# A mixture-of-experts kernel behind linear attention: layer 1 of all four experts in another seven-product form

## Chip, core and metric

One Trainium2 chip, of which the kernel uses one core. The metric is the device time of one execution in microseconds (us). Before the change it is 514.11 us, the median of three runs (513.86 to 515.35).

## What is computed

Linear attention feeds a small mixture of experts. The reference, cut to what matters:

```python
def phi(x): return np.where(x > 0, x, np.exp(x) - 1.0) + 1.0
q_p, k_p = phi(q), phi(k)                       # 8 batches, 8 heads, 576 tokens, 64 wide
kv  = einsum('bhsd,bhse->bhde', k_p, v); z = k_p.sum(axis=2)
x   = einsum('bhsd,bhde->bhse', q_p, kv) / (einsum('bhsd,bhd->bhs', q_p, z)[..., None] + 1e-6)
x   = x as (4608 tokens, 512)
p   = domain_probs / (domain_probs.sum(-1, keepdims=True) + 1e-9)
for e in range(4):
    h = np.maximum(x @ w1[e], 0.0)              # 512 -> 1024
    out += p[:, e:e+1] * (h @ w2[e])            # 1024 -> 512
```

## The kernel before

**Stages.** Attention of the first batches runs on its own, with its loads; the first 512 tokens of the experts (`first_l1`, `first_l2`) lie between its parts. The rest of the experts is cut into 64 units: `units` goes over j from 1 to 8 (512 tokens each), two halves s of 256 tokens, and the four experts e, which turn fastest. Beside the units, attention of batches 2 to 7 runs until about 370 us.

**One unit.** A unit is two token tiles of 128 (t = 0, 1) for one expert. ScalarE scales x by the token's share p into `xp` (L649, two instructions), the DMA queue of SyncE transposes it into `xT` (L651). Layer 1 makes h, layer 2 multiplies it with w2 and adds into four PSUM banks `l2b`, which stay open over the four experts; after expert 3 the output sums (L832 to L841) go to `ot` and to memory.

**Seven products.** Both layers are 2 x 2 block products: x as x[t, k] (token tile t, half k of the 512), w1 as quadrants q[f, k] (half f of the 1024, half k), h as h[t, f]. Eight block products give four results; with sums of blocks, seven do. A block product on TensorE is 8 matmuls of 128 columns. `l1_seven` does so for experts 0 to 2, with three PSUM banks that turn from unit to unit: the first product A is read by ScalarE, which writes its negative into bank W (L717), so that the third product adds onto it; the second, Bk, is copied to `m2` (L719). VectorE takes W - m2 to `w` (L722). Products four and five end in relus on ScalarE (L725, L728), six and seven in VectorE instructions that add `w` and cut off below zero (L731, L735). `l1_plain` does expert 3 with all eight block products (L747: 32 matmuls of 256 columns, four relus L766). Layer 2 is in seven products for all experts: `ssums` makes four sums of h on VectorE (L785), `l2_unit` seven products of four matmuls of 256 columns (L799), in the order that `seq` gives.

**Weight sums.** `sums_w1` makes on VectorE three new tiles `w1x` for each of the experts 0 to 2 and overwrites quadrants of w1 in place, six instructions in all (L487, L498). The in-place ones have to wait until the first 512 tokens, which use the plain w1, are through.

**Sums of x.** `xsums` (L661 to L668) makes five sums in three instructions for a unit of experts 0 to 2.

**What sets the order.** Everything is first noted in a plan: `pl.add(engine, duration, priority, function, reads, writes)`. `Plan.order` then plays the plan with these durations (0.45 us for a layer-1 product, 0.436 for a layer-2 one, 0.5 for a PSUM read on ScalarE, 0.55 for an x scaling, 0.62 for a VectorE read of PSUM) and 0.28 us from engine to engine. At each step the engine that can start first takes, of what is ready, the one with the lowest priority number. The result is a fixed order for each engine. Priorities are due times: unit n is due at

```python
T0, TU = 84.0, 6.4
U = lambda n: T0 + n * TU
```

a layer-1 product i of unit n at U(n) + 0.9 i, a layer-2 product i of the same unit at U(n+1) + 0.45 + 0.9 i, so that layer 1 of one unit interleaves with layer 2 of the one before. In fact an engine doesn't wait for a due time; it takes what is ready.

**Loads.** The first two batches use three staging buffers for k, q and v; the third lies on tiles that units use later (`w` and `m2`). Outputs turn over three `ot` tiles.

Of the kernel before, what the change touches and what calls it, by code (L numbers as in the profile page):

```python
# [10 lines left out]
FP32 = mybir.dt.float32  # L11
FP16 = mybir.dt.float16
# [97 lines left out]
def kernel(  # L110
# [16 lines left out]
    P = 128  # L127
# [10 lines left out]
    SEVEN1 = (0, 1, 2)  # L138
# [13 lines left out]
    w1x = {e: sb(f"w1x_{e}", [P, 3, 2, FH], FP16) for e in SEVEN1}  # L152
# [5 lines left out]
    xp_b = [sb(f"xp{i}", [P, 2, Dm], FP16) for i in range(2)]  # L158
    xT_b = [sb(f"xT{i}", [P, 2, DC, P], FP16) for i in range(3)]
    xs_b = [sb(f"xs{i}", [P, 5, 2, P], FP16) for i in range(2)]  # L160
    h_b = [sb(f"h{i}", [P, 2, 2, HF, P], FP16) for i in range(2)]
    s4_b = [sb(f"s4{i}", [P, 4, HF, P], FP16) for i in range(2)]
    m2_b = sb("m2", [P, 512], FP32)
    w_b = sb("w", [P, 2, 512], FP32)
    s15 = sb("s15", [P, 2, HD], FP32)
    ot_b = [sb(f"ot{i}", [P, 2, Dm], FP32) for i in range(3)]
# [17 lines left out]
    kqs.append(w_b.rearrange("p a (i h c d) -> p (a i) h c d", i=1, h=2, c=C))  # L184
    vss.append(m2_b.rearrange("p (h c d) -> p h c d", h=2, c=C))
# [24 lines left out]
    def stage_keys(i):  # L210

        if i < 2:
            return ("st", i, 0), ("st", i, 1), ("st", i, 2)
        return ("w", 0), ("w", 1), ("m2",)
# [61 lines left out]
    def probs():  # L276
        raw = sb("praw", [P, B, C, E], FP32)
        rrest = sb("prawr", [P, B // 2, E], FP32)
        src = moe_domain_probs.rearrange("(b s) e -> s b e", s=S)
        dma("POOL", 6, raw, src[0:NT].rearrange("(p c) b e -> p b c e", c=C), ("praw",), 1.5)  # L280
        for par in range(2):
            dma("POOL", 6, rrest[par * R : (par + 1) * R],
                src[NT:S].rearrange("s (b t) e -> t s b e", t=2)[par], (("prawr", par),), 0.4)

        def go(r, o, rs, nb):
            nc.vector.tensor_reduce(out=rs, in_=r, axis=mybir.AxisListType.X, op=AO.add)
            nc.vector.tensor_scalar(rs, rs, 1e-9, None, AO.add)
            nc.vector.reciprocal(rs, rs)
            nc.vector.scalar_tensor_tensor(
                out=o, in0=r, scalar=INV, in1=rs.broadcast_to([P, nb, E]),  # L290
                op0=AO.mult, op1=AO.mult,
            )

        rs0, rs1 = sb("prs0", [P, B * C], FP32), sb("prs1", [P, B // 2], FP32)
        pl.add("DVE", 0.6, 24, lambda: go(raw.rearrange("p b c e -> p (b c) e"),
               p_nat.rearrange("p b c e -> p (b c) e"), rs0, B * C), r=("praw",), w=("pnat",))
        pl.add("DVE", 0.4, 60, lambda: go(rrest, p_rest, rs1, B // 2),
               r=(("prawr", 0), ("prawr", 1)), w=("prest",))
# [179 lines left out]
    def sums_w1(e, pri):  # L478

        if e not in SEVEN1:  # L480
            return
# [7 lines left out]
        q00, q01, q10, q11 = wq(e, 0, 0), wq(e, 0, 1), wq(e, 1, 0), wq(e, 1, 1)  # L489
        for o, a, b_, alu, r, w in (  # L490
            (w1x[e][:, 2], q00, q01, AO.add, K(0, 0) + K(0, 1), (X(2),)),
            (w1x[e][:, 1], q10, q11, AO.add, K(1, 0) + K(1, 1), (X(1),)),
            (w1x[e][:, 0], q00, q11, AO.add, K(0, 0) + K(1, 1), (X(0),)),
            (q10, q10, q00, AO.subtract, K(0, 0), K(1, 0)),
            (q01, q01, q11, AO.subtract, K(1, 1), K(0, 1)),
        ):
            pl.add("DVE", 0.62, pri, two(o, a, b_, alu), r=r, w=w, after=22)
        pl.add("DVE", 0.4, pri, lambda: nc.vector.tensor_scalar(q00, q00, -1.0, None, AO.mult),  # L498
               r=(), w=K(0, 0))
# [155 lines left out]
    def xsums(n):  # L655
        if units[n][2] not in SEVEN1:
            return
# [3 lines left out]
        for i, (o, a, b_, alu, dur, d) in enumerate((  # L661
            (xs[:, 4], xT[:, 0, 0:2], xT[:, 1, 2:4], AO.add, 0.25, 1.8),
            (xs[:, 2:4], xT[:, :, 2:4], xT[:, :, 0:2], AO.subtract, 0.42, 2.7),
            (xs[:, 0:2].rearrange("p a k t -> p (a k) t"), xT[:, 0], xT[:, 1], AO.add, 0.42, 4.5),
        )):
            pl.add("DVE", dur, U(n) + d - 1.0,
                   lambda o=o, a=a, b_=b_, alu=alu: tt(out=o, in0=a, in1=b_, op=alu),  # L667
                   r=(("xT", ti),), w=(("xs", xi, i),))  # L668
# [4 lines left out]
    def l1_seven(n):  # L673
# [3 lines left out]
        i0 = rot("l1u", 3)  # L677
        cnt["l1u"] += 1
        ia, ib, iw = i0, (i0 + 1) % 3, (i0 + 2) % 3
        A, Bk, W = l1b[ia], l1b[ib], l1b[iw]  # L680
        ka, kb, kw = "l1b%d" % ia, "l1b%d" % ib, "l1b%d" % iw
        wi = n % 2
        w = w_b[:, wi]
        H = lambda t, f: ("h", n % 2, t, f)
        K = lambda i, kk: k1(e, i, kk)
        X = lambda i: ("w1x", e, i)

        def prod(bank, wt, r, start):
# [12 lines left out]
        t_ = (("xT", ti),)  # L701
        steps = (
            (A, ka, w1x[e][:, 2], (X(2),), xT[:, 1, 2:4], t_, True),
            (Bk, kb, w1x[e][:, 1], (X(1),), xT[:, 0, 0:2], t_, True),
            (W, kw, w1x[e][:, 0], (X(0),), xs[:, 4], x_(0), False),
            (A, ka, wq(e, 0, 0), K(0, 0), xs[:, 3], x_(1), False),
            (Bk, kb, wq(e, 1, 1), K(1, 1), xs[:, 2], x_(1), False),
            (A, ka, wq(e, 1, 0), K(1, 0), xs[:, 0], x_(2), False),
            (Bk, kb, wq(e, 0, 1), K(0, 1), xs[:, 1], x_(2), False),
        )  # L710
        for i, (bank, key, wt, wkey, r, rk, start) in enumerate(steps):
# [3 lines left out]
                   r=rk + wkey, w=(key,))  # L715
            if i == 0:
                pl.add("ACT", 0.5, p_ + 1.0, lambda: nc.scalar.mul(W, A, -1.0), r=(ka,), w=(kw,))  # L717
            elif i == 1:
                pl.add("ACT", 0.5, p_ + 1.0, lambda: nc.scalar.copy(m2_b, Bk),  # L719
                       r=(kb,), w=(("m2",),))  # L720
            elif i == 2:
                pl.add("DVE", 0.62, p_ + 1.5, lambda: nc.vector.tensor_tensor(  # L722
                    out=w, in0=W, in1=m2_b, op=AO.subtract), r=(kw, ("m2",)), w=(("w", wi),))
            elif i == 3:
                pl.add("ACT", 0.5, p_ + 0.9, lambda: nc.scalar.activation(  # L725
                    hq(n, 1, 0), A, AF.Relu), r=(ka,), w=(H(1, 0),))
            elif i == 4:
                pl.add("ACT", 0.5, p_ + 0.9, lambda: nc.scalar.activation(  # L728
                    hq(n, 0, 1), Bk, AF.Relu), r=(kb,), w=(H(0, 1),))
            elif i == 5:  # L730
                pl.add("DVE", 0.62, p_ + 0.5, lambda: nc.vector._custom_dve(  # L731
                    TENSOR_ADD_SAT, out=hq(n, 1, 1), in0=A, in1=w, s0=BIG, s1=0.0),
                    r=(ka, ("w", wi)), w=(H(1, 1),))
            else:
                pl.add("DVE", 0.62, p_ + 0.5, lambda: nc.vector._custom_dve(  # L735
                    TENSOR_ADD_SAT, out=hq(n, 0, 0), in0=Bk, in1=w, s0=BIG, s1=0.0),
                    r=(kb, ("w", wi)), w=(H(0, 0),))

    def l1_plain(n):
        j, s, e = units[n]  # L740
        ti = n % 3
        xT = xT_b[ti]
        h = h_b[n % 2]

        def prod(ph, fp, f2):
            for dc in range(DC):
                nc.tensor.matmul(  # L747
                    out=ph[:, f2 * 2 * P : (f2 + 1) * 2 * P],
                    lhsT=w1_sb[e][:, dc, (2 * fp + f2) * P : (2 * fp + f2 + 1) * P],
                    rhs=xT[:, :, dc, :],  # L750
                    start=(f2 == 0 and dc == 0),
                    stop=(dc == DC - 1),
                    skip_group_check=True,
                )

        for fp in range(FC // 2):
            bi = rot("l1u", 3)
            ph, key = l1b[bi], "l1b%d" % bi
            f, c0 = (2 * fp) // HF, (2 * fp) % HF
            for f2 in range(2):  # L760
                pl.add("PE", 0.436, U(n) + 1.6 * fp + 0.8 * f2,
                       lambda ph=ph, fp=fp, f2=f2: prod(ph, fp, f2),
                       r=(("xT", ti),) + k1(e, (2 * fp) // HF, 0) + k1(e, (2 * fp) // HF, 1),
                       w=(key,))
            pl.add("ACT", 0.52, U(n) + 1.6 * fp + 1.5,
                   lambda ph=ph, f=f, c0=c0: nc.scalar.activation(  # L766
                       h[:, :, f, c0 : c0 + 2, :],
                       ph.rearrange("p (c u t) -> p u c t", c=2, u=2),
                       AF.Relu), r=(key,), w=(("h", n % 2, 0, f), ("h", n % 2, 1, f)))
# [18 lines left out]
    def l2_unit(n):  # L788
# [26 lines left out]
        seq = (P2, P4, P1, P5, P6, P7, P3)  # L815
        if first:
            seq = (P2, P1, P5, P6, P7, P4, P3)
# [7 lines left out]
        oi = rot("ot", 3)  # L825
# [98 lines left out]
    for n in range(nu):  # L924
# [5 lines left out]
        (l1_seven if units[n][2] in SEVEN1 else l1_plain)(n)  # L930
# [45 lines left out]
```

## Time and profile before

| | |
|---|---|
| median of three runs | 514.11 us |
| the profiled execution | 514.07 us |
| its span, first to last instruction | 512.2 us |
| mean granted clock of TensorE | 0.996 |
| TensorE busy (PE) | 486.8 us |
| VectorE busy (DVE) | 411.8 us |
| ScalarE busy (ACT) | 333.7 us |
| first product of unit 0 starts | 85.1 us |
| last layer-2 product ends | 504.4 us |
| L691, 128-wide matmuls of seven-product layer 1 | 2688 |
| L747, 256-wide matmuls of plain layer 1 | 512 |

How to read it: the profile gives each engine's busy time, groups of instructions by source line with count, busy sum, mean duration in ns and the idle time before them, and who ended that idle time. The chain of work that ended last is followed back from the last instruction. A timeline row has the start, the duration, the engine, the line, what is written and read, and how many instructions it joins. A matmul's end is modelled and includes the drain of the pipeline, so back-to-back matmuls overlap in these rows; their starts tell the pace. PEld is the loading of weights, which lies under matmuls.

### The profile page before, as it was taken

The numbers are of one execution on the slowest core, as the hardware profiler recorded it, in microseconds if no ns is written. First come the engines' busy times: TensorE is split into PE (matmuls) and PEld (weight loads), VectorE is DVE, ScalarE is ACT, GpSimd is POOL, SyncE is SP. The second block draws the span as 40 slices with busy tenths as digits, with TensorE's granted clock in tenths as the row PEclk, the third lists the DMA queues.
The fourth block names the chain that finished last, engine by engine and source line by source line (L and its number), as shares of the span: only waits on it lengthen the run. The fifth ranks groups of instructions, "written<-read, shape, count | busy, mean of one in ns | idle before, by whom it ended". The sixth has DMA issues, their size and how long they took to land.

```text
span 512.2 us, 13906 instructions
## 1 busy us (share of the span) xinstructions
PE 486.8 (95%) x5624; PEld 424.3 (83%) x5624; DVE 411.8 (80%) x1005; ACT 333.7 (65%) x621; POOL 42.8 (8%) x68
## 2 busy tenths in 40 slices
PE   1889998999999999999999999999999999999993
PEld 0444544899999999999999999999999999999993
DVE  5887987989898989898989889888877675767652
ACT  5638568878885688658765886578546756565431
POOL 8756400000000000000000000000000000000000
PEclk9999999999999999999999999999999999999998
DMA  8999988996565587455745475735423224232211
GB/s 230 240 231 235 262 182 183 243 196 158 115 176 109 153 144 154 115 155 125 171 115 134 113 176 102 148 91 102 76 42 85 49 77 57 70 60 66 53 33 42
DMA packets 124001, 67.44 MB, mean 132 GB/s; under 512 B 94480, under 2 KB 117776, under 8 KB 123936
## 3 DMA queue, kind: packets, MB, share of 16 engines
q1 hardware_dynamic: 115216, 51.79, 46.4%
q0 software_dynamic: 8720, 14.76, 13.4%
q8 instruction: 44, 0.72, 0.6%
q14 instruction: 21, 0.17, 0.1%
HBM read 45.16 MB, written 9.44 MB: 107 GB/s over the span
## 4 chain that ended last, share of the span: by engine, by line
PE 90%; DVE 3%; ACT 2%; DMA 2%; issue 1%; POOL 0%; POOLq 0%; DVEq 0%; ACTq 0%
PE l2b L799 37%; PE l1b L691 28%; PE l1b L747 11%; PE l2b L547 5%; PE l1b L537 5%; PE at L421 2%; PE at L397 1%; DMA vr<-in_v_dram 1%; DMA xT<-xp 1%; DVE x L437 0%; ACT ek L355 0%; ACT xp L649 0%; PE l2b L367 0%; PE at L400 0%; DVE ot L839 0%
## 5 line engine op out<-in xcount | busy, mean ns | idle before, releaser
L691 PE MATMUL l1b<-xs,w 128*128 128x128 f16 x1536 | 116.0, 219 | 1.4 <-ACT h L725 1.4
L799 PE MATMUL l2b<-t,s 128*128 128x256 f16 x768 | 114.6, 273 | 0.1
L799 PE MATMUL l2b<-w,h 128*128 128x256 f16 x768 | 113.6, 273 | 0.2 <-DVE h L731 0.2
L691 PEld LDWEIGHTS <-w 128*128 128x128 f16 x1536 | 100.2, 98 | 5.3 <-issue 1.5
L799 PEld LDWEIGHTS <-s 128*128 128x128 f16 x1024 | 92.5, 98 | 7.8 <-DVE s L785 0.3
L649 ACT ACTIVATE xp<-x,p_nat 128x512 f16<-128x512 f16 x112 | 76.5, 719 | 3.4 <-DMA xT<-xp 3.2
L691 PEld LDWEIGHTS <-w1x 128*128 128x128 f16 x1152 | 75.2, 98 | 3.9 <-DVE xs L667 0.9
L785 DVE TENSOR_TENSOR s<-h 128x512 f16<-128x512 f16 x128 | 53.8, 420 | 27.7 <-ACT h L766 27.1
L799 PEld LDWEIGHTS <-h 128*128 128x128 f16 x768 | 69.5, 98 | 6.4 <-DVE h L731 0.3
L747 PE MATMUL l1b<-xT,w 128*128 128x256 f16 x512 | 74.0, 273 | 0.0
L766 ACT ACTIVATE h<-l1b 128x512 f16<-128x512 f32 x64 | 38.1, 595 | 45.8 <-PE l1b L747 40.4
L691 PE MATMUL l1b<-xT,w1x 128*128 128x128 f16 x768 | 57.6, 219 | 0.0
L747 PEld LDWEIGHTS <-w 128*128 128x128 f16 x512 | 49.6, 98 | 5.5
L667 DVE TENSOR_TENSOR xs<-xT 128x256 f16<-128x256 f16 x144 | 48.3, 374 | 6.8 <-PE l1b L691 4.7
L725 ACT ACTIVATE h<-l1b 128x512 f16<-128x512 f32 x48 | 28.5, 594 | 32.3 <-PE l1b L691 32.3
L717 ACT ACTIVATE l1b<-l1b 128x512 f32<-128x512 f32 x48 | 28.1, 586 | 21.3 <-PE l1b L691 15.5
L355 ACT ACTIVATE ek<-kq 128x512 f16<-128x512 f32 x60 | 37.6, 631 | 6.3 <-DVE kqp L348 2.5
L731 DVE CUSTOM_DVE_ANT_0 h<-l1b,w 128x512 f16<-128x512 f32 x48 | 32.9, 686 | 10.4 <-ACT h L728 5.0
L722 DVE TENSOR_TENSOR w<-l1b,m 128x512 f32<-128x512 f32 x48 | 32.9, 686 | 7.3 <-PE l1b L691 6.3
L799 PE MATMUL l2b<-w,s 128*128 128x256 f16 x256 | 38.4, 273 | 0.0
L735 DVE CUSTOM_DVE_ANT_0 h<-l1b,w 128x512 f16<-128x512 f32 x48 | 33.0, 687 | 2.1 <-PE l1b L691 0.9
L348 DVE TENSOR_TENSOR kqp<-ek,kqp 128x512 f16<-128x512 f16 x64 | 27.2, 426 | 9.0 <-ACT ek L355 5.2
(100 smaller groups left out, 621.0 us busy)
## 6 DMA issues: line engine op xcount, KB each, us to landing
w<-in_moe_w_dram POOLq DMA_DIRECT2D x32, 256.0 KB, 7.4
out_dram<-ot SPq DMA_DIRECT2D x16, 512.0 KB, 3.0
kq<-in_k_dram SPq DMA_DIRECT2D x25, 256.0 KB, 3.2
vs<-in_v_dram SPq DMA_DIRECT2D x25, 256.0 KB, 3.2
kq<-in_q_dram SPq DMA_DIRECT2D x25, 256.0 KB, 3.0
kq<-in_k_dram POOLq DMA_DIRECT2D x5, 256.0 KB, 7.2
vs<-in_v_dram POOLq DMA_DIRECT2D x5, 256.0 KB, 6.6
kq<-in_q_dram POOLq DMA_DIRECT2D x5, 256.0 KB, 6.1
```

What stands on the lines that cost most here:

```text
L355: pl.add("ACT", 0.55, pri + i * step, lambda i=i: nc.scalar.activation(ek[:, i], kq[:, i], AF.Exp), r=(sk[i],), w=(("ek", ei, i),))
L649: pl.add("ACT", 0.55, pri, lambda c=c, src=src, ps=ps: nc.scalar.activation(xp[:, c, :], src, AF.Copy, scale=ps), r=r, w=(("xp", xi, c),))
L667: lambda o=o, a=a, b_=b_, alu=alu: tt(out=o, in0=a, in1=b_, op=alu),
L691: nc.tensor.matmul(out=bank[:, fc * P : (fc + 1) * P], lhsT=wt[:, kc, fc * P : (fc + 1) * P], rhs=r[:, kc, :], start=(start and fc == 0 an ...
L722: pl.add("DVE", 0.62, p_ + 1.5, lambda: nc.vector.tensor_tensor(out=w, in0=W, in1=m2_b, op=AO.subtract), r=(kw, ("m2",)), w=(("w", wi),))
L725: pl.add("ACT", 0.5, p_ + 0.9, lambda: nc.scalar.activation(hq(n, 1, 0), A, AF.Relu), r=(ka,), w=(H(1, 0),))
L731: pl.add("DVE", 0.62, p_ + 0.5, lambda: nc.vector._custom_dve(TENSOR_ADD_SAT, out=hq(n, 1, 1), in0=A, in1=w, s0=BIG, s1=0.0), r=(ka, ("w", ...
L735: pl.add("DVE", 0.62, p_ + 0.5, lambda: nc.vector._custom_dve(TENSOR_ADD_SAT, out=hq(n, 0, 0), in0=Bk, in1=w, s0=BIG, s1=0.0), r=(kb, ("w" ...
L747: nc.tensor.matmul(out=ph[:, f2 * 2 * P : (f2 + 1) * 2 * P], lhsT=w1_sb[e][:, dc, (2 * fp + f2) * P : (2 * fp + f2 + 1) * P], rhs=xT[:, :, ...
L766: lambda ph=ph, f=f, c0=c0: nc.scalar.activation(h[:, :, f, c0 : c0 + 2, :], ph.rearrange("p (c u t) -> p u c t", c=2, u=2), AF.Relu), r=( ...
L785: pl.add("DVE", 0.36, U(n + 1) + d - 0.5, lambda i=i, a=a, b_=b_, alu=alu: tt(out=s4[:, i], in0=a, in1=b_, op=alu), r=r, w=(Q(i),))
L799: nc.tensor.matmul(out=l2b[bank][:, half * HD : (half + 1) * HD], lhsT=a[:, c, :], rhs=w[:, c], start=(opens and first and c == 0), stop=( ...
```

## The change

Layer 1 of all four experts takes one form of seven products, another than before, and `l1_plain` goes. With sums of weights

w1 = q10 + q11, w2 = w1 - q00, w4 = q01 - w2, and q10 overwritten by q00 - q10

(four instructions for each of four experts) and four sums of x in three instructions, each of which uses the one before, the seven products go into the banks X, Y, Z:

1. X = q00 x00; ScalarE copies X to Y.
2. Z = w1 xs0; ScalarE copies Z to `p5`.
3. X += w2 xs2; ScalarE copies X to `u2`.
4. Y += q01 x01; ScalarE: h[0,0] = relu(Y).
5. X += (q00 - q10) xs1; VectorE: h[1,1] = relu(X + p5).
6. Z += w4 x11; VectorE: h[1,0] = relu(Z + u2).
7. X += q11 xs3; ScalarE: h[0,1] = relu(X).

In the next unit X and Y change places. The subtraction L722 goes; ScalarE reads PSUM five times in a unit in place of four. Layer 2 takes its products in another order (P1 before P4 before P5). The third staging buffer lies on `xp` and `u2`, the raw probabilities on `p5`, and `ot` has two tiles in place of three. The core of the diff:

```diff
-    SEVEN1 = (0, 1, 2)
-    w1x = {e: sb(f"w1x_{e}", [P, 3, 2, FH], FP16) for e in SEVEN1}
+    w1x = [sb(f"w1x_{e}", [P, 3, 2, FH], FP16) for e in range(E)]
-    m2_b = sb("m2", [P, 512], FP32)
-    w_b = sb("w", [P, 2, 512], FP32)
+    u2_b = [sb(f"u2{i}", [P, 512], FP32) for i in range(2)]
+    p5_b = sb("p5", [P, 512], FP32)
-    ot_b = [sb(f"ot{i}", [P, 2, Dm], FP32) for i in range(3)]
+    ot_b = [sb(f"ot{i}", [P, 2, Dm], FP32) for i in range(2)]
...
+            (w1, q10, q11, AO.add, K(1, 0) + K(1, 1), (X(0),)),
+            (w2, w1, q00, AO.subtract, (X(0),) + K(0, 0), (X(1),)),
+            (w4, q01, w2, AO.subtract, (X(1),) + K(0, 1), (X(2),)),
+            (q10, q00, q10, AO.subtract, K(0, 0), K(1, 0)),
...
+            (xs[:, 0:2], xT[:, 1].rearrange("p (a k) t -> p a k t", a=2), xT[:, :, 0:2],
+             0.42, 0.9, (), (X(0), X(1))),
+            (xs[:, 2], xT[:, 1, 2:4], xs[:, 0], 0.25, 1.8, (X(0),), (X(2),)),
+            (xs[:, 3], xT[:, 0, 2:4], xs[:, 2], 0.25, 5.4, (X(2),), (X(3),)),
...
+        ix, iy, iz = cnt.get("l1u", (0, 1, 2))
+        cnt["l1u"] = (iy, ix, iz)
...
+            (X, kx, wq(e, 0, 0), k1(e, 0, 0), xT[:, 0, 0:2], t_, True,
+             ("ACT", 0.5, 1.0, copy(Y, X), (kx,), (ky,))),
+            (Z, kz, w1, S_(0), xs[:, 0], x_(0), True,
+             ("ACT", 0.5, 2.5, copy(p5_b, Z), (kz,), ("p5",))),
+            (X, kx, w2, S_(1), xs[:, 2], x_(2), False,
+             ("ACT", 0.5, 1.0, copy(u2, X), (kx,), (("u2", ui),))),
+            (Y, ky, wq(e, 0, 1), k1(e, 0, 1), xT[:, 0, 2:4], t_, False,
+             ("ACT", 0.5, 2.0, relu(hq(n, 0, 0), Y), (ky,), (H(0, 0),))),
+            (X, kx, wq(e, 1, 0), k1(e, 1, 0), xs[:, 1], x_(1), False,
+             ("DVE", 0.62, 0.9, relu2(hq(n, 1, 1), X, p5_b), (kx, "p5"), (H(1, 1),))),
+            (Z, kz, w4, S_(2), xT[:, 1, 2:4], t_, False,
+             ("DVE", 0.62, 1.2, relu2(hq(n, 1, 0), Z, u2), (kz, ("u2", ui)), (H(1, 0),))),
+            (X, kx, wq(e, 1, 1), k1(e, 1, 1), xs[:, 3], x_(3), False,
+             ("ACT", 0.5, 1.0, relu(hq(n, 0, 1), X), (kx,), (H(0, 1),))),
...
-        seq = (P2, P4, P1, P5, P6, P7, P3)
+        seq = (P1, P4, P5, P2, P6, P7, P3)
         if first:
-            seq = (P2, P1, P5, P6, P7, P4, P3)
+            seq = (P1, P5, P2, P6, P7, P4, P3)
...
-        oi = rot("ot", 3)
+        oi = rot("ot", 2)
```

The third number in each tuple after "ACT" or "DVE" is how long after the product's due time the reader is due.

More of the change, by code (lines that the diff above doesn't have):

```diff
@@ L156 @@
     p_rest = sb("p_rest", [P, B // 2, E], FP32)
-    xp_b = [sb(f"xp{i}", [P, 2, Dm], FP16) for i in range(2)]
+    xp_a = sb("xp", [P, 2, 2, Dm], FP16)
+    xp_b = [xp_a[:, i] for i in range(2)]
     xT_b = [sb(f"xT{i}", [P, 2, DC, P], FP16) for i in range(3)]
-    xs_b = [sb(f"xs{i}", [P, 5, 2, P], FP16) for i in range(2)]
+    xs_b = [sb(f"xs{i}", [P, 4, 2, P], FP16) for i in range(2)]
     h_b = [sb(f"h{i}", [P, 2, 2, HF, P], FP16) for i in range(2)]
     s4_b = [sb(f"s4{i}", [P, 4, HF, P], FP16) for i in range(2)]
-    m2_b = sb("m2", [P, 512], FP32)
-    w_b = sb("w", [P, 2, 512], FP32)
+    u2_b = [sb(f"u2{i}", [P, 512], FP32) for i in range(2)]
+    p5_b = sb("p5", [P, 512], FP32)
     s15 = sb("s15", [P, 2, HD], FP32)
-    ot_b = [sb(f"ot{i}", [P, 2, Dm], FP32) for i in range(3)]
+    ot_b = [sb(f"ot{i}", [P, 2, Dm], FP32) for i in range(2)]
     kqs = [sb(f"kq{i}", [P, 2, 2, C, D], FP32) for i in range(2)]
@@ L182 @@
     xr_sb = sb("xr_sb", [P, B // 2, Dm], FP16)
-    kqs.append(w_b.rearrange("p a (i h c d) -> p (a i) h c d", i=1, h=2, c=C))
-    vss.append(m2_b.rearrange("p (h c d) -> p h c d", h=2, c=C))
+    kqs.append(
+        xp_a.bitcast(FP32).rearrange("p a c (x d) -> p a (c x) d", d=D)
+        .rearrange("p a (h c) d -> p a h c d", h=2)
+    )
+    vss.append(u2_b[0].rearrange("p (h c d) -> p h c d", h=2, c=C))
     xt0 = s4_b[1].rearrange("p a c t -> p a (c t)")
@@ L213, in stage_keys @@
             return ("st", i, 0), ("st", i, 1), ("st", i, 2)
-        return ("w", 0), ("w", 1), ("m2",)
+        return ("xp", 0), ("xp", 1), ("u2", 0)
     last = {}
@@ L276, in probs @@
     def probs():
-        raw = sb("praw", [P, B, C, E], FP32)
+        raw = p5_b[:, 0 : B * C * E].rearrange("p (b c e) -> p b c e", b=B, c=C)
         rrest = sb("prawr", [P, B // 2, E], FP32)
         src = moe_domain_probs.rearrange("(b s) e -> s b e", s=S)
-        dma("POOL", 6, raw, src[0:NT].rearrange("(p c) b e -> p b c e", c=C), ("praw",), 1.5)
+        dma("POOL", 6, raw, src[0:NT].rearrange("(p c) b e -> p b c e", c=C), ("p5",), 1.5)
         for par in range(2):
@@ L295, in probs @@
         pl.add("DVE", 0.6, 24, lambda: go(raw.rearrange("p b c e -> p (b c) e"),
-               p_nat.rearrange("p b c e -> p (b c) e"), rs0, B * C), r=("praw",), w=("pnat",))
+               p_nat.rearrange("p b c e -> p (b c) e"), rs0, B * C), r=("p5",), w=("pnat",))
         pl.add("DVE", 0.4, 60, lambda: go(rrest, p_rest, rs1, B // 2),
@@ L478, in sums_w1 @@
     def sums_w1(e, pri):
-        if e not in SEVEN1:
-            return
         tt = nc.vector.tensor_tensor
@@ L489, in sums_w1 @@
         q00, q01, q10, q11 = wq(e, 0, 0), wq(e, 0, 1), wq(e, 1, 0), wq(e, 1, 1)
+        w1, w2, w4 = (w1x[e][:, i] for i in range(3))
         for o, a, b_, alu, r, w in (
[L491 to L495, printed above, removed]
+            (w1, q10, q11, AO.add, K(1, 0) + K(1, 1), (X(0),)),
+            (w2, w1, q00, AO.subtract, (X(0),) + K(0, 0), (X(1),)),
+            (w4, q01, w2, AO.subtract, (X(1),) + K(0, 1), (X(2),)),
+            (q10, q00, q10, AO.subtract, K(0, 0), K(1, 0)),
         ):
             pl.add("DVE", 0.62, pri, two(o, a, b_, alu), r=r, w=w, after=22)
-        pl.add("DVE", 0.4, pri, lambda: nc.vector.tensor_scalar(q00, q00, -1.0, None, AO.mult),
-               r=(), w=K(0, 0))
     def sums_w2(e, pri):
@@ L655, in xsums @@
     def xsums(n):
-        if units[n][2] not in SEVEN1:
-            return
         xi, ti = n % 2, n % 3
@@ L660, in xsums @@
         tt = nc.vector.tensor_tensor
[L661 to L664, printed above, removed]
+        X = lambda i: ("xs", xi, i)
+        for i, (o, a, b_, dur, d, r, w) in enumerate((
+            (xs[:, 0:2], xT[:, 1].rearrange("p (a k) t -> p a k t", a=2), xT[:, :, 0:2],
+             0.42, 0.9, (), (X(0), X(1))),
+            (xs[:, 2], xT[:, 1, 2:4], xs[:, 0], 0.25, 1.8, (X(0),), (X(2),)),
+            (xs[:, 3], xT[:, 0, 2:4], xs[:, 2], 0.25, 5.4, (X(2),), (X(3),)),
         )):
             pl.add("DVE", dur, U(n) + d - 1.0,
-                   lambda o=o, a=a, b_=b_, alu=alu: tt(out=o, in0=a, in1=b_, op=alu),
-                   r=(("xT", ti),), w=(("xs", xi, i),))
+                   lambda o=o, a=a, b_=b_: tt(out=o, in0=a, in1=b_, op=AO.subtract),
+                   r=(("xT", ti),) + r, w=w)
     def hq(n, t, f):
@@ L676, in l1_seven @@
         xT, xs = xT_b[ti], xs_b[xi]
[L677 to L683, printed above, removed]
+        ix, iy, iz = cnt.get("l1u", (0, 1, 2))
+        cnt["l1u"] = (iy, ix, iz)
+        X, Y, Z = l1b[ix], l1b[iy], l1b[iz]
+        kx, ky, kz = "l1b%d" % ix, "l1b%d" % iy, "l1b%d" % iz
+        ui = n % 2
+        u2 = u2_b[ui]
         H = lambda t, f: ("h", n % 2, t, f)
-        K = lambda i, kk: k1(e, i, kk)
-        X = lambda i: ("w1x", e, i)
+        S_ = lambda i: (("w1x", e, i),)
         def prod(bank, wt, r, start):
@@ L701, in l1_seven, with relu, copy, relu2 @@
         t_ = (("xT", ti),)
-        steps = (
[L703 to L709, printed above, removed]
+        w1, w2, w4 = (w1x[e][:, i] for i in range(3))
+        def relu(o, bank):
+            return lambda: nc.scalar.activation(o, bank, AF.Relu)
+        def copy(o, bank):
+            return lambda: nc.scalar.copy(o, bank)
+        def relu2(o, bank, t):
+            return lambda: nc.vector._custom_dve(
+                TENSOR_ADD_SAT, out=o, in0=bank, in1=t, s0=BIG, s1=0.0
+            )
+        steps = (
+            (X, kx, wq(e, 0, 0), k1(e, 0, 0), xT[:, 0, 0:2], t_, True,
[12 more added lines that the diff above has]
+             ("ACT", 0.5, 1.0, relu(hq(n, 0, 1), X), (kx,), (H(0, 1),))),
         )
-        for i, (bank, key, wt, wkey, r, rk, start) in enumerate(steps):
+        for i, (bank, key, wt, wk, r, rk, start, then) in enumerate(steps):
             p_ = U(n) + 0.9 * i
@@ L714, in l1_seven @@
                    lambda bank=bank, wt=wt, r=r, start=start: prod(bank, wt, r, start),
[L715 to L769, printed above, removed]
@@ L771, in ssums @@
+                   r=rk + wk, w=(key,))
+            eng, dur, d, f, r, w = then
+            pl.add(eng, dur, p_ + d, f, r=r, w=w)
     def ssums(n):
@@ L929 @@
         xsums(n)
-        (l1_seven if units[n][2] in SEVEN1 else l1_plain)(n)
+        l1_seven(n)
         ssums(n)
```

## Prediction

> **What bounds the kernel now.** I read the busy shares first, then the waits of TensorE, then busy time by stretch, then the timeline of single units, last the rows of the instructions that the change adds and removes.
>
> ```profile
> PE 486.8 (95%) x5624; PEld 424.3 (83%) x5624; DVE 411.8 (80%) x1005; ACT 333.7 (65%) x621; POOL 42.8 (8%) x68
> ...
> PE 90%; DVE 3%; ACT 2%; DMA 2%; issue 1%; POOL 0%; POOLq 0%; DVEq 0%; ACTq 0%
> ```
>
> TensorE (PE) is busy for 95% and carries 90% of the chain that ended last. The waits of PE show where the rest goes:
>
> ```profile
> PE l1b L691 <- ACT h L725: 1.4, 1, 1.4
> ...
> PE l1b L691 <- DVE xs L667: 0.8, 1, 0.8
> ```
>
> These two, both in unit 0, are all that layer 1 waited for (waits under 150 ns aren't listed). Busy time by stretch (PE, weight loads, VectorE = DVE, ScalarE = ACT):
>
> ```profile
> 185.00:210.00 25.00, 25.00 (x323) 23.46 (x321) 22.36 (x59) 21.42 (x40) 0.00 (x0) 1.00 0.71 142
> 210.00:235.00 25.00, 25.00 (x319) 23.44 (x318) 21.77 (x55) 15.46 (x31) 0.00 (x0) 1.00 0.49 129
> ...
> 435.00:460.00 25.00, 25.00 (x313) 23.32 (x311) 17.10 (x40) 14.53 (x25) 0.00 (x0) 1.00 0.26 61
> ```
>
> PE has no gap, at full granted clock (1.00). While attention runs beside the units (to about 370 us) DVE is at 88% and ACT at 62 to 86%; after that 68% and 58%. So a shorter PE stream shortens the span, unless ACT or DVE is then late.
>
> **What goes from PE.** Two stretches of PE's timeline, a seven-product unit and a plain one:
>
> ```profile
> 221.59 0.61 PE L691 MATMUL l1b<-xs,w 128*128 128x128 f16 x8
> 222.04 0.60 PE L799 MATMUL l2b<-t,s 128*128 128x256 f16 x4
> 222.47 0.61 PE L691 MATMUL l1b<-xs,w 128*128 128x128 f16 x8
> ...
> 210.05 0.60 PE L747 MATMUL l1b<-xT,w 128*128 128x256 f16 x4
> 210.49 0.60 PE L799 MATMUL l2b<-w,h 128*128 128x256 f16 x4
> 210.92 0.60 PE L747 MATMUL l1b<-xT,w 128*128 128x256 f16 x4
> ```
>
> Starts are 0.44 us apart in both; the 0.6 us contain the pipeline's drain. From start to start a 128-wide matmul takes 55.8 ns (mean over the 336 products of L691), a 256-wide one 109.1 ns (L747). A seven-product layer 1 is 7 x 8 x 55.8 = 3.13 us, a plain one 32 x 109.1 = 3.49 us: 0.366 us less, in the 16 units of expert 3 = **5.9 us**. Check: without attention a seven-product unit starts 6.18 us after the one before it (400.42 to 406.60), and a seven-product plus a plain one take 12.74 us, so the plain one takes 6.56, 0.38 more.
>
> [...] I take 5.9 us.
>
> **What ACT and DVE get.** Their rows:
>
> ```profile
> L719 ACT COPY m<-l1b 128x512 f32<-128x512 f32 x48 | 28.1, 585 | 5.2 <-PE l1b L691 5.1
> L731 DVE CUSTOM_DVE_ANT_0 h<-l1b,w 128x512 f16<-128x512 f32 x48 | 32.9, 686 | 10.4 <-ACT h L728 5.0
> L667 DVE TENSOR_TENSOR xs<-xT 128x512 f16<-128x512 f16 x96 | 38.1, 420 | 4.9 <-PE l1b L691 4.7
> L667 DVE TENSOR_TENSOR xs<-xT 128x256 f16<-128x256 f16 x48 | 13.6, 284 | 1.9 <-DMA xT<-xp 1.8
> ```
>
> DVE, old seven-product unit: sums of x 284 + 2 x 420, subtraction L722 686, two relu sums 2 x 687, four sums of h 4 x 420: 4.86 us; plain unit only 1.68. New unit: 420 + 2 x 284 + 1374 + 1680 = 4.04 us. Four units (one per expert) take 3 x 4.86 + 1.68 = 16.26 before and 16.17 after: the same work, spread evenly. In an attention-phase period (26.25 us, now 25.9) DVE goes from 89% to 90%.
>
> ACT: four reads of PSUM in any old unit, five in a new one, so +585 ns x 4 = 2.3 us per four units and 64 x 0.585 = 37 us in all. Attention stretches between 110 and 385 us average 18.0 us busy in 25 (72%), which becomes (18.9 + 2.3)/25.9 = 82%; later 58% becomes about 66%. The fullest old stretch (86%) would reach some 95%. None of this is on PE's path by itself.
>
> Weight sums on DVE: 9 + 6 of about 685 ns and 3 of 485 (11.7 us) become 16 of 685 (11.0 us). The four of expert 3 (2.7 us) are new between 76 and 104 us. Three write only new tiles and fit where DVE idles there (2.6, 0.8 and 0.8 us between 76 and 82 us); the fourth overwrites a quadrant and must wait for PE's first-tile products. Units 0 to 2 also ask 0.82 us less of DVE each. I cost it at nothing; uncovered it is 2.7 us.
>
> **What is added as waits.** Bank X gets four products with a reader after each: copy to Y, copy to u2, relu sum on DVE, relu. Three links are tight: the next product on X stands two layer-1 slots on, 1.77 us (4 x 0.44) after its predecessor's start. The nearest rows are the old links of the same kind:
>
> ```profile
> 216.89 0.61 PE L691 MATMUL l1b<-xT,w1x 128*128 128x128 f16 x8
> 217.68 0.60 ACT L717 ACTIVATE l1b<-l1b 128x512 f32<-128x512 f32 x1
> 218.83 0.61 PE L691 MATMUL l1b<-xs,w1x 128*128 128x128 f16 x8
> ```
>
> The product ends at 217.50, ACT starts 0.18 us later, and the product that needs the seed starts 0.55 us after its end. Over the 48 old units ACT started 0.04 to 0.18 us (medians) after such a product and by 0.34 to 0.53 in nine of ten; the shortest time from ACT's end to PE's next use is 0.05 us. So an ACT link takes 0.61 + 0.04 + 0.59 + 0.05 = 1.29 us and bears 0.48 us of queueing. The DVE link (relu sum between the fifth and seventh product; old relu sums start 0.14 to 0.18 us after their product, nine of ten by 0.46) takes 0.61 + 0.14 + 0.69 + 0.05 = 1.49 and bears 0.28. Behind a late link stand, in PE's order, the layer-2 products of the unit before and the attention products; behind a late PE, all readers. The chain through a unit (relu and copy to Y 1.91 + 1.29 + 1.49) is 4.7 us of the 6.18 that PE needs: not the bound while ACT and DVE are prompt. A random arrival in the attention phase would find ACT or DVE busy with one instruction longer than these margins in about 14% of cases, by 0.1 us on average then: 0.013 us a link over all arrivals, 2.5 us for three links in 64 units. The planner, though, puts ACT's reads at 0.5 us and x scaling at 0.55 against 0.59 and 0.72 measured, so in a full stretch ACT falls behind its plan, and its order is fixed. Lower end: nothing, as in the old units 1 to 47; upper end: 0.3 us a unit in the 41 attention units, 12 us. Not below nothing: the change takes no wait from PE that it has. I take **2 us**, near the lower end because the old tight links at 72% ACT lost nothing.
>
> Head and tail: unit 0 has no layer 2 to lie beside it. Old waits there are 1.4 and 0.8 us; new, the second product needs a sum of x (the old third one did), DVE starts those at 86.6 us, so the X chain runs bare from there: third product at about 87.4, fifth at 88.7, seventh at 90.2 us, the next unit at 90.6 (old: 90.8). Level, within 1 us. In the tail the bank with P1 and P5 closes earlier (P5 third, not fourth), but PE still ends with P3: -0.3 us at best. Two output tiles for three: each is reused after some 50 us, its store lands in 3; nothing. The stage that lay on w and m2 now lies on xp and u2: its last use ends at 54.5 us, x scaling starts at 73.3; nothing.
>
> Sum: 514.07 (profiled execution; span 512.2, 1.9 around it, and the median of the runs is 514.11) - 5.9 + 2.0 - 0.3 = 509.9.
>
> **Rivals.** First, the whole gain: the planner places every link and nothing is late; 514.1 - 5.9 - 0.3 = 507.9. For it: layer 1 waited nowhere after unit 0. Against: ACT has a fifth reader and three links in a row. Second, the gain is eaten: about 0.09 us of lateness a unit (5.9/64) makes no difference, 512.6 to 515.6. Third, slower: the X chain becomes the bound in the attention phase, because ACT there runs near 95% in full stretches by longer instructions than planned, and a copy behind an exp (0.63) and an x scaling (0.72) is 0.8 us late. The place is the third and fifth product of units 0 to 41; it decides from 0.14 us a unit (5.9/41). At 0.3 us: 514.1 - 5.9 + 12.3 = 520.5. Against it: ACT now has 7 us idle in 26 there, and loses 2.3. That the change doesn't do what it says would show as L747 still running; the diff leaves no plain unit.
>
> **How the numbers follow.** Forecast (508.5 to 512.5) 0.50, whole gain 0.12, eaten 0.15, slower 0.23. About 0.3% (1.5 us) is what a measurement here can tell from no change: faster 0.62, same 0.15, slower 0.23. Range 507.4 to 519.0: it leaves out half of the slower case and the end of the whole gain.[...]
>
> **What would show it.** Right: PE without gaps from 110 us, period of four units 25.9 us with attention and 24.7 without, no 256-wide layer 1, ACT up by some 37 us, DVE level. Wrong: waits of layer-1 products on the copies or the DVE relu sum over some 4 us in all, or 128-wide matmuls off 55.8 ns, or unit 3 waiting for expert 3's weight sums.

## The result and the profile after

The changed kernel takes 508.74 us (median of four runs, 507.95 to 510.41), the old one beside it 514.73: ratio 0.9888 with a 95% interval of 0.9856 to 0.9920. The forecast was 509.9, faster with a chance of 0.62. Beside each other a second time (e9 below) they took 508.91 and 513.53, ratio 0.9909 (0.9892 to 0.9925). The profiled execution took 510.41 us, at the upper end of its runs; the reason is in the start and is shown below.

The lines of the page after that answer to those of before, busy time and the chain:

```profile
PE 484.1 (95%) x6008; PEld 425.0 (84%) x6008; DVE 410.6 (81%) x1035; ACT 367.1 (72%) x685; POOL 42.6 (8%) x68
...
PE 85%; ACT 5%; DMA 4%; DVE 2%; issue 2%; POOL 0%; POOLq 0%; DVEq 0%; ACTq 0%
```

ACT has 33.4 us more busy time (forecast 37; the durations of its rows do add up to 37.3 us more, but rows overlap, and busy time counts an overlap once), DVE 1.2 us less (forecast level). Layer 1's only listed waits on PE are again two, both in unit 0:

```profile
PE l1b L689 <- ACT l1b L706: 0.7, 1, 0.7
PE l1b L689 <- DVE h L709: 0.4, 1, 0.4
```

The same stretches as before (PE, weight loads, DVE, ACT):

```profile
185.00:210.00 25.00, 24.90 (x343) 23.51 (x341) 22.82 (x61) 23.25 (x44) 0.00 (x0) 1.00 0.83 158
210.00:235.00 25.00, 25.00 (x348) 23.77 (x346) 21.68 (x57) 17.35 (x34) 0.00 (x0) 1.00 0.54 133
...
435.00:460.00 25.00, 25.00 (x342) 23.70 (x340) 16.96 (x41) 17.15 (x30) 0.00 (x0) 1.00 0.28 64
```

PE is still without gaps, but for a tenth of a microsecond in the fullest stretches, as here, where ACT now stands at 93%. In the timeline of PE after attention two units follow each other like this:

```profile
423.42 0.60 PE L765 MATMUL l2b<-w,s 128*128 128x256 f16 x4
423.86 0.61 PE L689 MATMUL l1b<-xT,w 128*128 128x128 f16 x8
424.31 0.60 PE L765 MATMUL l2b<-w,h 128*128 128x256 f16 x4
424.74 0.61 PE L689 MATMUL l1b<-xs,w1x 128*128 128x128 f16 x8
```

Every unit now starts 6.18 us after the one before (417.68, 423.86, 430.04), four take 24.73 us without attention and 25.89 with it (217.97 to 243.86): the forecast said 24.7 and 25.9. A 128-wide matmul still takes 55.8 ns from start to start.

**Where the time went, from the two profiled executions.** "Idle" is the time from start to start on PE above what a matmul of that width takes when nothing holds it (55.8 ns at 128 columns, 109.1 at 256).

| us | before | after | difference |
|---|---|---|---|
| span | 512.2 | 508.6 | -3.6 |
| start to first product of unit 0 | 85.1 | 87.3 | +2.2 |
| from there to the end of layer 2 | 419.3 | 414.0 | -5.3 |
| of it PE idle before 110 us / to 370 us / later | 3.5 / 0.5 / 0.4 | 3.7 / 1.2 / 0.1 | +0.6 |
| end of layer 2 to the end | 7.8 | 7.4 | -0.5 |

The middle is what the change does: 5.9 us less work on PE, 0.6 us more idle time. The second row, the later start, is something else. The first 512 tokens' 16 matmuls of 512 columns, before and after (PE's timeline), and one stretch in which they lie, before and after (the value ahead of the last two is the granted clock):

```profile
28.57 3.61 PE L537 MATMUL l1b<-s,w 128*128 128x512 f16 x16
```

```profile
29.78 4.59 PE L537 MATMUL l1b<-s,w 128*128 128x512 f16 x16
```

```profile
28.40:31.70 3.30, 3.26 (x16) 1.46 (x15) 2.55 (x5) 3.02 (x7) 1.69 (x3) 1.00 1.19 204
```

```profile
28.40:31.70 3.30, 3.30 (x9) 1.21 (x8) 2.95 (x5) 2.07 (x4) 2.01 (x4) 0.50 1.16 205
```

For 3.4 us (28.3 to 31.7) the clock is 0.50 of full speed and about half as many matmuls run. That costs the 16 matmuls 1.0 us and the three ahead of them 0.5; the other 0.7 us of the later start lie before it (those three start at 28.21 us, before at 27.51). No run shows what sets it off; in the 3.4 us ahead (24.9 to 28.3) the clock was 1.00 and PE busy for 1.7 us (in the same stretch before: 1.00 and 2.1).

The half clock seems to go with the execution, not with the change. Of the profiled executions of the other runs below, e1, e4, e8 and e9 have a mean clock of 0.991 to 0.994 (the changed kernel's has 0.994), and from 28 to 32 us e1 and e9 stand at 0.55 to 0.59 (the changed kernel's at 0.57 and 0.58). e2, e3, e5, e6, e7 and e10 have a mean of 0.995 to 0.997 (the old kernel's has 0.996), and from 28 to 32 us e3, e7 and e10 stand at 1.00; e7, with the same work up to unit 0 as the changed kernel, starts unit 0 at 85.2 us. The other three executions of the changed kernel took 1.6 to 2.5 us less than the profiled one. And of 23 executions of the old kernel beside e1, the five slowest (515.49 to 516.71 us) have a mean clock of 0.992 or 0.993, and the others took at most 514.74 at (but for one) 0.994 to 0.998, so it probably meets this in some executions too; no trace of those is kept.

### The profile page after: what moved, and what is told of

Same layout as the page of the kernel before. It is cut to its first block, busy times and chain, and to the rows that moved or that the text cites. A ratio compares the mean times of both kernels' runs of the same rounds, so it can differ in the third digit from the quotient of the medians.

```text
span 508.6 us, 14922 instructions
## 1 busy us (share of the span) xinstructions
PE 484.1 (95%) x6008; PEld 425.0 (84%) x6008; DVE 410.6 (81%) x1035; ACT 367.1 (72%) x685; POOL 42.6 (8%) x68
## 4 chain that ended last, share of the span: by engine, by line
PE 85%; ACT 5%; DMA 4%; DVE 2%; issue 2%; POOL 0%; POOLq 0%; DVEq 0%; ACTq 0%
PE l1b L689 37%; PE l2b L765 36%; PE l2b L547 4%; PE l1b L537 4%; DMA kq<-in_k_dram 2%; PE at L424 2%; PE at L400 1%; DMA kqr<-in_q_dram 1%; ACT xp L649 1%; ACT ek L358 1%; DMA w<-in_moe_w_dram 1%; ACT h L703 1%; ACT l1b L706 1%; ACT p L706 0%; DVE x L440 0%
## 5 line engine op out<-in xcount | busy, mean ns | idle before, releaser
L709 DVE CUSTOM_DVE_ANT_0 h<-l1b,p 128x512 f16<-128x512 f32 x64 | 44.2, 691 | 50.1 <-PE l1b L689 48.5
L689 PE MATMUL l1b<-xT,w 128*128 128x128 f16 x1024 | 78.1, 219 | 0.8 <-ACT l1b L706 0.7
L689 PE MATMUL l1b<-xs,w1x 128*128 128x128 f16 x1024 | 77.9, 219 | 0.9 <-DVE h L709 0.4
L689 PE MATMUL l1b<-xs,w 128*128 128x128 f16 x1024 | 78.0, 219 | 0.0
L706 ACT COPY u<-l1b 128x512 f32<-128x512 f32 x64 | 37.5, 586 | 16.0 <-PE l1b L689 15.8
L709 DVE CUSTOM_DVE_ANT_0 h<-l1b,u 128x512 f16<-128x512 f32 x64 | 43.7, 682 | 0.8 <-ACT h L703 0.5
L706 ACT COPY l1b<-l1b 128x512 f32<-128x512 f32 x64 | 36.8, 575 | 10.4 <-PE l1b L689 9.6
L706 ACT COPY p<-l1b 128x512 f32<-128x512 f32 x64 | 37.3, 583 | 7.9 <-PE l1b L689 6.7
L667 DVE TENSOR_TENSOR xs<-xT,xs 128x256 f16<-128x256 f16 x128 | 37.0, 289 | 5.1 <-PE l1b L689 0.5
L537 PE MATMUL l1b<-s,w 128*128 128x512 f16 x124 | 31.1, 399 | 1.4 <-ACT s L532 1.2
```

Source lines behind the costliest of these rows:

```text
L537: nc.tensor.matmul(out=bank, lhsT=w1_sb[e][:, dc, fj * P : (fj + 1) * P], rhs=xt0[:, dc, :], start=(dc == 0), stop=(dc == DC - 1),)
L667: lambda o=o, a=a, b_=b_: tt(out=o, in0=a, in1=b_, op=AO.subtract),
L689: nc.tensor.matmul(out=bank[:, fc * P : (fc + 1) * P], lhsT=wt[:, kc, fc * P : (fc + 1) * P], rhs=r[:, kc, :], start=(start and fc == 0 an ...
L706: return lambda: nc.scalar.copy(o, bank)
L709: return lambda: nc.vector._custom_dve(TENSOR_ADD_SAT, out=o, in0=bank, in1=t, s0=BIG, s1=0.0)
```

## The experiments

**e1: expert 3 plain again, the rest in the new form.** It takes expert 3's 16 units back alone; the sums of weights and of x that only they need go with them. The core of the edit:

```diff
-        l1_seven(n)
+        (l1_plain if units[n][2] == 3 else l1_seven)(n)
```

> New form for experts 0 to 2 only; expert 3 is plain again (32 matmuls of 256 columns), as before the change. Theory PE (the gain is the 0.366 us that each of expert 3's 16 units loses on TensorE, nothing else): the whole gain goes, within 1 us of the old kernel, ratio 1.000. Rival (the gain is in the form itself, by its evener VectorE work, fewer sums and the shorter tail): about half of it stays, 511 to 512 us, ratio below 0.996.

Measured: 514.69 us, ratio 1.0008 (0.9993 to 1.0023). From the first product of unit 0 to the end of layer 2 it takes 419.3 us, as the old kernel does. All of the gain is in expert 3's units; the rest of the change taken together (the new form for experts 0 to 2, the order of layer 2, the tiles that moved) is worth nothing that can be measured while PE sets the pace. The rival falls.

**e2 and e5: the old form for all four experts.** Same matmuls on PE as in the change, 0.8 us more on DVE in each unit, 0.6 less on ACT. To make room, `w` has one buffer in place of two and some tiles move. The core of the edit:

```diff
-    SEVEN1 = (0, 1, 2)
+    SEVEN1 = (0, 1, 2, 3)
-    w_b = sb("w", [P, 2, 512], FP32)
+    w_b = sb("w", [P, 1, 512], FP32)
```

> The old seven-product form for all four experts (PE has the same matmuls as in the changed kernel; VectorE has 0.8 us more in each unit and ScalarE one read less). To make room, w has one buffer, the third stage lies on xp and m2, the raw probabilities on m2, ot has two tiles. By durations of the rows VectorE then has 26.5 us of work in a period of 25.9 with attention. Theory A (VectorE is bound by the sum of its rows' durations, so the new form is needed): VectorE sets the pace in the attention phase, 514 to 517 us, ratio about 1.00. Theory B (back-to-back instructions overlap by some 0.08 us, so that VectorE has room): 508.5 to 510.5 us, ratio about 0.99, so that four experts in seven products are the gain and the form hardly matters.

Measured: 521.18 us, ratio 1.0137 (1.0122 to 1.0151). In this kernel the raw probabilities and a v of attention reach their common tile in the wrong order, so it computes with other data, and PE waits 6.1 us at once in the first tokens for a copy of x. e5 has the right order and is otherwise the same.

> The old seven-product form for all four experts once more, with the raw probabilities and the third stage's v in the right order on their common tile. Theory A (VectorE, 0.8 us more a unit than in the new form, becomes the bound): 518 to 522 us, with PE idle in the attention phase and VectorE above 94% there. Theory B (the form hardly matters, the 521 us came from the wrong order of the loads at the start): 508.5 to 511 us.

Measured: 515.60 us, ratio 1.0024 (1.0013 to 1.0034), between the two forecasts: the wrong order explains 5.6 us of e2, and 6.9 us over the changed kernel remain. Its stretches:

```profile
285.00:310.00 25.00, 24.50 (x330) 22.78 (x329) 24.07 (x63) 19.99 (x39) 0.00 (x0) 1.00 0.52 119
...
435.00:460.00 25.00, 25.00 (x342) 23.68 (x340) 20.08 (x46) 15.06 (x26) 0.00 (x0) 1.00 0.32 65
```

DVE stands at 96% with attention, and PE loses half a microsecond in 25; at 80% later it loses nothing. In all PE is idle 11.3 us in this kernel against 5.0 in the changed one, 6.4 us more, which is nearly all of the measured difference. Theory A points to the right engine: the sum of rows forecast 26.5 us of DVE work in a period of 25.9. It overstates the size, since back to back DVE's instructions start sooner than their rows last (a relu sum 0.61 us after the one before, row 0.69; a sum of h 0.34, row 0.42).

That DVE's load is the cause is argued, not isolated. PE's listed waits between 110 and 375 us are for DVE and for ACT:

```profile
PE l2b L803 <- DVE h L739: 0.8, 2, 0.4
PE l1b L695 <- ACT l1b L721: 0.8, 2, 0.5
```

ACT is only 59 to 80% busy there, so it is late by the order of its work, perhaps behind a late DVE. The single buffer `w` is a rival that no run separates; as VectorE alone writes and reads it, it adds no wait between engines, but it binds the order of DVE's work. What is shown is that four experts in the old form, with these tiles, lose the gain, and in the new form keep it.

**e3: one more read on ACT in every unit.** This prices the rival on the slower side.

```diff
             eng, dur, d, f, r, w = then
             pl.add(eng, dur, p_ + d, f, r=r, w=w)
+            if i == 1:
+                pl.add(eng, dur, p_ + d, f, r=r, w=w)
```

> Changed kernel with the copy to p5 issued twice in every unit (same data): 0.59 us more on ScalarE a unit, 91% busy in the attention phase. Theory PE (links have room): under 1 us more than the changed kernel, ratio to the old one at most 0.991. Rival (ScalarE is at its edge and its lateness reaches PE over the X bank's links): 0.14 us or more a unit in the 41 attention units, 6 to 12 us, ratio 1.00 or more.

Measured: 513.76 us, ratio 0.9988 (0.9974 to 1.0002): 5.0 us more than the changed kernel, just under the rival's range and far from the forecast "under 1 us". Waits of PE, and two neighbouring stretches:

```profile
PE l1b L689 <- ACT u L706: 2.0, 6, 0.4
PE l1b L689 <- ACT l1b L706: 1.6, 4, 0.7
```

```profile
185.00:210.00 25.00, 24.33 (x328) 22.43 (x326) 21.34 (x57) 24.24 (x47) 0.00 (x0) 1.00 0.76 154
210.00:235.00 25.00, 25.00 (x348) 23.78 (x346) 22.29 (x58) 19.18 (x39) 0.00 (x0) 1.00 0.55 135
```

The waits are those of the X bank, at the third product (for the copy to Y) and the fifth (for the copy to u2), where the prediction's third rival put them, and mostly in every other stretch, where attention fills ACT to 96 to 98%. PE's idle time from 110 to 370 us rises from 1.2 to 4.7 us, and before 110 us from 3.7 to 4.9; together that is 4.8 of the 5.0 us. So the rival's mechanism is real; the change stops short of its point.

**e6: half of that.** The second copy only for experts 0 and 2 (`if i == 1 and e % 2 == 0`).

> Changed kernel with the copy to p5 issued twice for experts 0 and 2 only: 0.29 us a unit on ScalarE on average, half of what cost 5.0 us. If lateness grows in proportion: 2.5 us over the changed kernel, 511.2. If ScalarE has a margin that only its fullest stretches pass (a knee): 0.3 to 1.2 us over it, 509 to 510.

Measured: 510.34 us, ratio 0.9918 (0.9904 to 0.9932): 1.6 us more than the changed kernel, between the two forecasts. The medians are from different chips and the intervals of the ratios overlap (e9: 0.9892 to 0.9925), but the traces agree: from unit 0's first product to the end of layer 2 it takes 415.7 us, the changed kernel 414.0. About half of that is before 110 us; from 110 to 370 us PE's idle time rises by 0.9 us, against 3.5 in e3, so beside attention the second half of the extra work costs about three times the first. The share of busy time alone doesn't tell when it starts to cost. In e6 ACT is as full as in e3, and PE has no gap in the profile's count (0.3 us from start to start):

```profile
185.00:210.00 25.00, 25.00 (x343) 23.52 (x342) 22.38 (x60) 24.50 (x47) 0.00 (x0) 1.00 0.74 154
```

**e4: one more sum on DVE in every unit.** The last sum of h is issued twice (the same `if` with `i == 3` in `ssums`).

> Changed kernel with the last sum of h issued twice in every unit (same data): 0.42 us more on VectorE a unit, 96% busy by durations in the attention phase. Theory PE: under 1 us more than the changed kernel. Rival (VectorE is at its edge: the relu sum between the fifth and the seventh product comes late): 4 to 10 us more, ratio 0.997 to 1.01.

Measured: 508.73 us, ratio 0.9892 (0.9878 to 0.9907), no difference from the changed kernel (508.74). DVE is 93 to 95% busy in every stretch with attention, and PE's idle time from 110 to 370 us is 1.3 us, as in the changed kernel (1.2). One of the stretches:

```profile
285.00:310.00 25.00, 25.00 (x346) 23.65 (x344) 23.60 (x62) 23.24 (x45) 0.00 (x0) 1.00 0.62 148
```

DVE has room for 0.42 us a unit. e5 asks 0.8 us more and is 6.9 us slower, but in another form, where the waits lie elsewhere; so an edge between the two is likely, not shown.

**e7: layer 2's products in the old order.** The edit for experts 1 to 3; the order for expert 0 goes back likewise.

```diff
-        seq = (P1, P4, P5, P2, P6, P7, P3)
+        seq = (P2, P4, P1, P5, P6, P7, P3)
```

> Changed kernel with layer 2's products in the old order (P2, P4, P1, P5 ...). In the new form h[0,1], which P2 needs, comes last. Theory (the planner's order and PE's other work hide it, only the tail changes): 508.7 to 509.7 us, up to 0.5 us of it in the tail. Rival (P2 first is late in each unit): 0.3 us a unit in waits of layer 2 for the relu, 520 us or more.

Measured: 510.95 us, ratio 0.9933 (0.9919 to 0.9948): 2.2 us more, outside both forecasts. From unit 0's first product to the end of layer 2 it takes 416.2 us against 414.0, the same 2.2 us, in small gaps of PE, 1.6 us of it between 110 and 370 us; the listed waits for the relu are 0.9 us in two places. So the new order, which takes the result that comes last, h[0,1], later, belongs to the change.

**e8, e9, e10: the idle time in the start.** e8 has unit 0 due earlier, e10 also a truer duration for the x scaling, e9 is the changed kernel beside e10.

```diff
-    T0, TU = 84.0, 6.4
+    T0, TU = 70.0, 6.4
```

> Changed kernel with unit 0 due at 70 in place of 84 us, so that the planner lets unit 0 lie beside the end of the first 512 tokens. TensorE stands 3.6 us in all between the first unit's start and 110 us. If that idle time is a matter of order: 1 to 2.5 us faster than the changed kernel, 506.5 to 507.7. If it is set by data (transposed x, sums on VectorE, x scaling on ScalarE): the same within 0.7 us, or slower by what attention's shifted due times cost.

> The changed kernel itself once more, beside the next one on the same chip: 508.2 to 509.2 us, and a narrower interval for its ratio, 0.988 to 0.990. Its profile also tells whether the start of unit 0 (85.1 us before, 87.3 us after) belongs to the kernel or to the execution: to the kernel if it is at 87.3 again, to the execution if it is near 85.2.

> The kernel with unit 0 due at 70 us, and the planner told 0.62 us in place of 0.55 for an x scaling, which is what one takes from start to start when ScalarE is full (0.61). If the few late copies left in the attention phase come from the planner's too short x scaling: 1 us less than with 0.55, near 507. If they come from attention's own instructions in front: no difference, 507.5 to 508.5.

Measured: e8 507.91 us, ratio 0.9869 (0.9854 to 0.9884); e9 508.91, ratio 0.9909 (0.9892 to 0.9925); e10 506.72, ratio 0.9865 (0.9850 to 0.9880). In e8 PE's idle time before 110 us falls from 3.7 to 2.5 us; the gain of 0.8 us falls between the two forecasts, and its interval overlaps that of the changed kernel's first measurement. e9's time is as forecast, its ratio just above. In e9 unit 0 starts at 87.3 us again, which by its forecast would make the late start the kernel's own; but e9's profile has the half clock again (0.55 and 0.59 in the two halves of 28 to 32 us), and the runs named above speak for the execution. e10 stands clear of e9, which ran beside it: 2.2 us faster. PE's idle time from 110 to 370 us is 0.5 us, against 1.6 in e8 and 1.3 in e9; about 1.5 us by which its profiled execution is faster than e9's come from the clock, which stayed at 1.00 from 28 to 32 us (an estimate, from the 1.5 us that the half clock cost in the profile after). That the duration alone does something isn't settled: e8 and e10 did not run side by side, and their ratios agree. e10 is the fastest of these kernels.

## Why the prediction was right

**PE's work (5.9 us): right.** 16 units lost 0.366 us each; e1 puts the 5.9 back. A 128-wide matmul takes 55.8 ns from start to start after as before, and the weight loads, 98 ns each, lie under other matmuls.

**Stalls by the new links (2 us): right in kind, too large.** PE's idle time from unit 0 on rose by 0.6 us. The links ran as the old rows said: ACT starts the copy to Y 0.17 us after its product (median, nine of ten by 0.58), the copy to u2 after 0.04 (0.50), DVE the relu sum after 0.14 (0.31). What is left after 110 us are four late links, 0.15 us at 110.1 and 0.26 to 0.28 us at 141.6, 187.0 and 290.8 us; the estimate had about one link in seven late, by 0.1 us each. The one at 141.6, in the timeline of ACT and of PE:

```profile
140.85 0.62 ACT L354 CAST vp<-vs 128x512 f16<-128x512 f32 x1
...
141.36 0.60 ACT L706 COPY l1b<-l1b 128x512 f32<-128x512 f32 x1
...
142.01 0.61 PE L689 MATMUL l1b<-xs,w1x 128*128 128x128 f16 x8
```

The first product of this unit ended at 140.42; relu and a cast of attention stood ahead of the copy, and the third product starts 0.05 us after its end.

**One argument was wrong.** The prediction said that ACT falls behind its plan because the planner counts 0.5 us for a read of PSUM that the row gives as 0.59. But rows overlap:

```profile
142.41 0.57 ACT L706 COPY p<-l1b 128x512 f32<-128x512 f32 x1
142.88 0.60 ACT L706 COPY u<-l1b 128x512 f32<-128x512 f32 x1
143.35 0.61 ACT L798 COPY s<-l2b 128x512 f32<-128x512 f32 x1
```

Three reads start 0.47 us apart. When ACT is full a copy takes 0.48 us from start to start, a relu 0.49, an x scaling 0.61 (medians), so the planner is right about the reads and only short about x scaling (0.55). A read's row overlaps the next instruction's by 0.10 us (median): of the 0.58 us of a copy's row, 0.48 pass before the next start. So ACT had more room than the prediction gave it: beside attention (110 to 385 us) it went from 72% to 80%, forecast 82%, and in its fullest stretch to 94%, forecast some 95%.

**DVE level (nothing): right** at the size, and e4 shows the room. The prediction's balance of DVE work did not ask what four experts in the old form would do; e5 did not keep the gain.

**Weight sums, stage, output tiles (nothing): no sign of a cost.** PE has no listed wait for a weight sum, in unit 3 or elsewhere. Unit 0 was level, as forecast: 5.6 us from its first product to unit 1's, 5.7 before. The tail gave 0.5 us, forecast 0.3. With the terms as measured the sum is 514.1 - 5.9 + 0.6 - 0.5 = 508.3, near the median of 508.7; the number was not right by luck.

**Rivals.** Whole gain (507.9): closer to the median than the forecast's own number, since the stalls are a third of what was forecast. Slower: its mechanism and place exist, but one more read of ACT a unit is needed to make the kernel about as slow as before. The prediction had set its point at 0.14 us of lateness a unit; e3 reached 0.12 on the same count (5.0/41) and stopped just short of it.

## What to carry to other kernels

Where one engine is busy without gaps, count its instructions from start to start; the change is worth what it takes from there, if the others keep up. Whether they do shows in their fullest stretches, not in their mean: here ACT at 72% on the page was up to 94% full beside attention, and one further instruction a unit gave five sixths of the gain back. Look at the waits there as well as at the share, since ACT at 97 to 98% cost PE 0.7 to 1.5 us per 25 us in e3 and 0.1 to 0.3 in e6. Two forms with the same matmuls can differ in time by more than the gain, here 6.9 us against 6.0 (e5), so count what each asks of the engines beside.

## What was not expected of the hardware

TensorE's clock fell to 0.50 for 3.4 us in the start of the profiled execution of the changed kernel, was at 0.55 and 0.59 in the two halves of 28 to 32 us in its second one (e9), and stayed at 1.00 there in that of the old one. What sets it off isn't shown; in the profile after, it hides 1.5 us of the gain. And two instructions of one engine that follow each other at once overlap in their rows by 0.08 (DVE) to 0.10 us (ACT), so here a sum of rows overstates what an engine is asked for: DVE took 0.42 us more a unit at no cost, though its rows from 110 to 360 us then add up to 106% of the time (e4).
